# Fused memory attention and gated feed-forward: two visits to the halved array per quad of heads in place of three, and a third P tile

## The chip, the cores and the metric

One core of a Trainium2 chip runs the whole kernel. The metric is device time in microseconds for one execution; lower is better.

## The reference, cut to what matters

Two branches share the input x (2048 x 640, float32) and are mixed by a gate per row.

```python
q, k, v = x@wq, x@wk, x@wv            # 32 heads of 20, 4 segments of 512 rows
for s in range(4):                    # per segment and head
    logits = qs @ ks.T * 20**-0.5 + causal_mask
    a_dot  = softmax(logits) @ vs
    a_mem  = (phi(qs) @ M) / (phi(qs) @ z + 1e-6)
    o      = g * a_mem + (1 - g) * a_dot        # g = sigmoid(beta), per head
    M, z   = M + phi(ks).T @ vs, z + phi(ks).sum()
a = o @ wo
b = (silu(x@w1) * (x@w3)) @ w2        # 640 -> 1728 -> 640
out = gate * a + (1 - gate) * b       # gate = sigmoid(x . gate_w)
```

## The kernel before, in words

All matmuls go through TensorE (PE), whose order is the order of the program; the other engines' orders are chosen by a scheduler when the program is built. Two streams share PE.

**The projection stream** is made of generators: q, k and v blocks, the memory's read and write, feed-forward up (`g`, `u`) and down (`f`), and the output projection (`op`). Inputs and weights are split into a high and a low part (`split`: a cast on ACT, L115, and a subtraction on POOL, L116), and each product takes three passes over 5 blocks, so one group is 15 matmuls of 128 rows into one PSUM bank. A generator yields some hundreds of nanoseconds of planned work at a time, and `step` takes the next piece.

**The attention stream** (`attention`) walks over 128 (segment, head) units in quads of 4, that is two pairs. Each of its passes m has 40 slots (L722 and on), and the main loop (L932 and on) takes projection pieces in each slot, as much as the plan's credit allows. In some slots, listed in `VISITS`, the stream visits PE. A pair has its two heads at partitions 0 and 64 of one `qk` tile, so their matmuls run side by side on the two halves of the array's rows. For a quad there are

- five `s_fill`s: logits q by k, two PSUM banks each, from which VectorE takes row maxima (L579);
- `max_rows`: the maxima are split, turned and written by four small DMAs of POOL's queue (L595) into two more rows of the `qk` tiles, so that the next product already has the maximum subtracted;
- five `t_fill`s: logits k by q, two banks each; ACT takes the exponential into the pair's P tile (L613), POOL zeroes what the mask excludes (L617);
- one `pv_quad`: P times V for four heads, 32 matmuls (L627), each using 32 of the array's columns, into one bank; the result is copied out (L631) to `oq`, which has one buffer, and stored to DRAM (L633). It is read back later as `oall`.

A fill holds 512 columns per half: one full block, or two or more smaller ones. Before the change the three visits of pass m are: slot 5 with s 0 and s 1 of quad m, `pv_quad` of quad m-2, t 0 and t 1 of quad m-1; slot 17 with s 2, t 2, s 4; slot 29 with s 3, t 3, t 4. The loads of the next quad (`load_pair`) stand at slots 20 and 36. P has two tiles, tag `P32`.

PSUM's 8 banks are handed out in turn by `bank_tile`: a free bank is taken from the front of the list and put back at its end; a bank of a projection group in progress is kept out of the list (`held`) until `filled` returns it. A bank that is handed out again makes PE wait until its last reader is done. Before a visit the main loop goes on with up to 4 pieces of projection work, until the open group has come far enough.

Of the kernel before, what the change touches and what calls it, by code (L numbers as in the profile page):

```python
# [25 lines left out]
BIG = -1.0e38  # L26
NST, NW, NRAW, NHT, NVG, NB = 4, 6, 2, 6, 2, 8
RH, LEAD = 3 * DH, 20
NP, AGE = 2, 4
LAG = 5  # L30
EARLY = range(2, 6)
OUT = {4: (0,), 5: (1,), 6: (2, 3)}
# [5 lines left out]
def gated_mix(ctx: ExitStack, tc: tile.TileContext, xT, wqk, wv, w13, w2, w2h, wo, beta, out):  # L38
    nc = tc.nc
# [8 lines left out]
    od = [dp.tile([H, 32, L], F32, name=f"od{c}") for c in range(NSEG)]  # L48
# [69 lines left out]
    free, held = list(range(NB)), {}  # L118

    def bank_tile(name, hold=None):  # L120


        k = free.pop(0)
        ps = pp.tile([P, L], F32, tag=f"b{k}", name=name, bufs=1)
        if hold:
            held[k] = -hold
        else:
            free.append(k)
        return ps
# [146 lines left out]
    def stores(now=False):  # L276
        for e in list(late):
            e[0] -= 1
            if now or e[0] <= 0:
                e[4].dma_start(e[1], e[2])  # L280
                stored.add(e[3])
                late.remove(e)
# [167 lines left out]
    def job_q(cs, mb, alloc={}):  # L450
        i = w_add(wqk[mb], D)
        return [(3.5, q_block(c, mb, i, alloc.get(c))) for c in cs]

    def job_q2(cs, mb, alloc={}):

        i = w_add(wqk[mb], D)
        j = w_add(wqk[mb + 1], D)
        return [(3.5, q_block(c, m, k, alloc.get(c), j if c == cs[-1] and m > mb else i))
                for c in cs for m, k in ((mb, i), (mb + 1, j))]
# [80 lines left out]
    def load_pair(p):  # L540

        j = 2 * p
        c, h = divmod(j, H)
        t = qk[p % NST]
        for mb in {DH * h // P, (DH * h + 2 * DH - 1) // P}:
            assert ("q", c, mb) in stored and ("k", c, mb) in stored
        assert ("v", c, 3) in stored
        for i in range(2):
            here(nc.gpsimd.dma_start(t[64 * i:64 * i + RH], qkd[c][RH * (h + i):RH * (h + i + 1)]))
        if h % 8 == 0:  # L550
            bank["v"] = v = vg[j // 8 % NVG]
            here(nc.sync.dma_start(v[:, :, :VG], vd[c][:, :, VE * h:VE * h + VG]))
        if p % 2 == 0:
            bank["m"] = sp.tile([P, 16], F32, tag="m", name=f"m{j}", bufs=2)
        for i in range(2):
            o = VE * (h % 8 + i)
            heads[j + i] = dict(c=c, h=h + i, v=bank["v"][:, :, o:o + 32])
        pairs[p] = dict(t=t, m=bank["m"])
# [63 lines left out]
    def pv_quad(p):  # L622

        ps = bank_tile(f"o{p}")
        for kb, (o, n) in enumerate(PSEG):
            for i in range(4):
                nc.tensor.matmul(ps[32 * i:32 * i + 32, kb * P:], heads[2 * p + i]["v"][:, kb],  # L627
                                 pairs[p + i // 2]["P"][:, i % 2, o:o + n],
                                 start=kb == 0, stop=kb == 3, skip_group_check=True)
        ot = sp.tile([P, L], F32, tag="oq", name=f"oq{p}", bufs=1)  # L630
        nc.scalar.copy(ot, ps)  # L631
        c, h = heads[2 * p]["c"], heads[2 * p]["h"]
        nc.scalar.dma_start(od[c][h:h + 4].rearrange("h e n -> (h e) n"), ot)  # L633
        q = p // 2 % 8
        for b in OUT.get(q, ()):
            after(8, o_load, c, b)
        if q == 7:
            after(6 if c < NSEG - 1 else 2, o_sums, c)
# [63 lines left out]
    def after(n, f, *a):  # L702
        soon.append([n, f, a])

    def tick():
        for e in list(soon):
            e[0] -= 1
            if e[0] <= 0:
                soon.remove(e)
                e[1](*e[2])  # L710

    NQUAD = NJ // 4


    VISITS = {5: (("s", 0, 0), ("s", 0, 1), ("o", 2), ("t", 1, 0), ("t", 1, 1)),
              17: (("s", 0, 2), ("t", 1, 2), ("s", 0, 4)), 29: (("s", 0, 3), ("t", 1, 3), ("t", 1, 4))}

    def attention():

        for m in range(-1, NQUAD + 2):  # L720
            for n in range(40):
                if m == -1 and n < 40 - LEAD:  # L722
                    continue

                todo = VISITS.get(n, ()) if m != 1 else {5: VISITS[5][:2], 9: VISITS[5][3:]}.get(n, VISITS.get(n, ()))
                if todo:
                    yield "visit"
                    for kind, q, *f in todo:
                        if 0 <= m - q < NQUAD:
                            if kind == "o":  # L730
                                pv_quad(2 * (m - q))
                            else:
                                (s_fill if kind == "s" else t_fill)(m - q, *f)
                    if n == 29 and 0 <= m < NQUAD:
                        after(4, max_rows, 2 * m)
                elif n in ((20, 34) if m < 0 else (20, 36)) and m + 1 < NQUAD:
                    load_pair(2 * (m + 1) + (n > 20))
                tick()
                yield m

# [132 lines left out]
    q = job_q(B[:1], 0, {2: big_tile})  # L873
# [5 lines left out]
    q = job_q2(B, 3)  # L879
# [20 lines left out]
    for n, (_, g) in enumerate(head):  # L900
# [7 lines left out]
        elif n == 9:  # L908
            gates()
    stores(True)  # L910
    att = attention()

    def begin():

        end, seg = segs.pop(0)
        n = end * 10 + LEAD - slots
        return [end, (d for _, g in seg for d in g), sum(c for c, _ in seg) * 1e3 / n]

    def step(run):
        d = next(run[1], None)  # L920
        if d is not None:
            for k in held:
                held[k] += d
            if not isinstance(d, float):
                stores()
                w_step()
        return d
# [3 lines left out]
    while run:  # L931
        if slots == run[0] * 10 + LEAD:  # L932
            while step(run) is not None:
                pass
            stores(True)
            run = begin() if segs else None
            continue
        if next(att, None) == "visit":

            for _ in range(4):  # L940
                if max(held.values(), default=-1) >= 0:
                    break
                d = step(run)
                if d is None:
                    break
                credit -= d
            next(att)
        slots += 1
        credit += run[2]
        while credit > 0:  # L950
            d = step(run)
            if d is None:
                if not segs:
                    break
                stores(True)
                run = begin()
                continue
            credit -= d
# [56 lines left out]
```

## Time and profile before

| what | value |
|---|---|
| median of 3 runs | 1116.74 us (1116.02 to 1117.21) |
| span of the profiled execution (no other time of it is given) | 1117.6 us |
| PE busy | 1105.9 us, 99% |
| PE weight loads busy | 903.6 us, 81% |
| DVE, ACT, POOL busy | 576.4, 475.8, 543.6 us |
| granted TensorE clock, mean | 0.997 |

PE's rows are read by their starts: in a row of the timeline that merges n matmuls, the first number is the first start, the second the time to the end of the last. Matmuls overlap (one takes 400 ns, the next starts before it ends), so PE shows as busy also where the next matmul starts later than it could; idle time in a table does not show it, the distance between starts does.

### The profile page before, as it was taken

The numbers are of one execution on the slowest core, as the hardware profiler recorded it, in microseconds if no ns is written. First come the engines' busy times: TensorE is split into PE (matmuls) and PEld (weight loads), VectorE is DVE, ScalarE is ACT, GpSimd is POOL, SyncE is SP. The second block draws the span as 40 slices with busy tenths as digits, with TensorE's granted clock in tenths as the row PEclk, the third lists the DMA queues.
The fourth block names the chain that finished last, engine by engine and source line by source line (L and its number), as shares of the span: only waits on it lengthen the run. The fifth ranks groups of instructions, "written<-read, shape, count | busy, mean of one in ns | idle before, by whom it ended". The sixth has DMA issues, their size and how long they took to land.

```text
span 1117.6 us, 19428 instructions
## 1 busy us (share of the span) xinstructions
PE 1105.9 (99%) x6953; PEld 903.6 (81%) x6953; DVE 576.4 (52%) x1718; ACT 475.8 (43%) x988; POOL 543.6 (49%) x731
## 2 busy tenths in 40 slices
PE   9999999999999999999999999999999999999998
PEld 6988887877877888878977776788778778877988
DVE  5022474355555554556244566874556665651544
ACT  6265334544244243265355644535543354344040
POOL 4153346466366353445264446645764555465140
PEclk8999999999999999999999999999999999999999
DMA  8265843334254323525377866446644333442122
GB/s 303 96 218 202 277 120 84 92 101 114 67 139 116 81 57 119 144 86 176 111 240 238 273 207 165 108 116 186 176 122 107 83 104 104 110 120 76 49 60 95
DMA packets 85808, 152.00 MB, mean 136 GB/s; under 512 B 19920, under 2 KB 32720, under 8 KB 85712
## 3 DMA queue, kind: packets, MB, share of 16 engines
q1 hardware_dynamic: 55920, 95.01, 26.6%
q0 software_dynamic: 22880, 41.86, 15.1%
q10 hardware_dynamic: 6912, 13.90, 3.3%
q8 instruction: 55, 0.90, 0.3%
q14 instruction: 41, 0.34, 0.1%
HBM read 95.25 MB, written 54.53 MB: 134 GB/s over the span
## 4 chain that ended last, share of the span: by engine, by line
PE 89%; issue 3%; DVE 2%; DMA 2%; POOL 2%; ACT 1%; SPq 0%; POOLq 0%; ACTq 0%; DVEq 0%
PE f L523 17%; PE g L261 16%; PE u L261 15%; PE q L261 6%; PE o L627 6%; PE k L261 6%; PE v L372 5%; PE s L572 5%; PE op L769 5%; PE t L607 4%; PE nd L339 2%; PE pm L426 1%; DMA qk<-mr 1%; POOL W L116 1%; DVE junk L579 1%
## 5 line engine op out<-in xcount | busy, mean ns | idle before, releaser
L579 DVE CUSTOM_DVE_ANT_0 junk<-s,mask 128x384 bf16<-128x384 f32 (+3 forms) x512 | 250.9, 490 | 136.9 <-PE s L572 102.2
L116 POOL TENSOR_TENSOR W<-wr,W 128x640 fp32r<-128x640 f32 (+1 forms) x126 | 197.6, 1573 | 194.8 <-ACT W L115 155.1
L613 ACT ACTIVATE P<-t 128x512 f32<-128x512 f32 (+1 forms) x384 | 171.6, 535 | 101.1 <-PE t L607 101.0
L617 POOL TENSOR_SCALAR_AFFINE_SELECT P<-P 128x256 f32<-128x256 f32 (+1 forms) x192 | 93.4, 493 | 248.5 <-ACT P L613 246.2
L261 PE MATMUL g<-X,W 128*128 128x512 f32 x840 | 213.8, 400 | 0.0
L523 PE MATMUL f<-W,ht 128*128 128x320 f32 x1312 | 202.5, 312 | 0.3 <-POOL W L116 0.3
L261 PE MATMUL u<-X,W 128*128 128x512 f32 x780 | 199.1, 400 | 0.7 <-DVE m L579 0.7
L523 PEld LDWEIGHTS f<-W,ht 128*128 128x128 f32 x1312 | 194.4, 189 | 4.3 <-POOL W L116 0.6
L261 PEld LDWEIGHTS g<-X,W 128*128 128x128 f32 x840 | 154.4, 188 | 36.7
L261 PEld LDWEIGHTS u<-X,W 128*128 128x128 f32 x780 | 143.6, 188 | 35.4 <-DVE m L579 1.2
L115 ACT CAST W<-wr 128x640 fp32r<-128x640 f32 (+1 forms) x133 | 95.4, 731 | 92.1 <-PE u L261 29.8
L531 DVE SCALAR_TENSOR_TENSOR acc<-f,cgate,acc 128x320 f32<-128x320 f32 x128 | 69.4, 548 | 42.5 <-PE f L523 42.0
L116 POOL TENSOR_TENSOR ht<-ft,ht 128x512 fp32r<-128x512 f32 x52 | 67.0, 1289 | 47.9 <-ACT ht L115 47.6
L595 POOL DMA_DIRECT2D qk<-mr x128 | 73.3, 575 | 31.1 <-DVE mr L590 24.4
L261 PE MATMUL q<-X,W 128*128 128x512 f32 x300 | 77.4, 411 | 1.5 <-ACT X L115 0.7
L261 PE MATMUL k<-X,W 128*128 128x512 f32 x300 | 76.8, 402 | 0.0
L492 DVE SCALAR_TENSOR_TENSOR fu<-ft,g 128x512 f32<-128x512 f32 x52 | 35.7, 687 | 77.7 <-ACT ft L491 69.0
L627 PE MATMUL o<-P,vg 128*32 128x512 f32 (+3 forms) x1024 | 75.5, 436 | 0.0
L769 PE MATMUL op<-W,oT 128*128 128x320 f32 x480 | 75.2, 313 | 0.0
L769 PEld LDWEIGHTS op<-W,oT 128*128 128x128 f32 x480 | 71.2, 189 | 1.6
L372 PE MATMUL v<-W,X 128*128 128x320 f32 (+1 forms) x480 | 71.8, 311 | 0.0
L372 PEld LDWEIGHTS v<-W,X 128*128 128x128 f32 x480 | 71.1, 189 | 0.4
(106 smaller groups left out, 1115.9 us busy)
## 6 DMA issues: line engine op xcount, KB each, us to landing
qk<-qkd POOLq DMA_DIRECT2D x128, 240.0 KB, 3.9
wr<-in_w_dram SPq DMA_DIRECT2D x80, 320.0 KB
qkd<-qs SPq DMA_DIRECT2D x20, 512.0 KB
qkd<-ks SPq DMA_DIRECT2D x20, 512.0 KB
od<-oq ACTq DMA_DIRECT2D x32, 256.0 KB
wr<-in_wo_dram SPq DMA_DIRECT2D x20, 320.0 KB
vg<-vd SPq DMA_DIRECT2D x16, 336.0 KB
xr<-in_xT_dram SPq DMA_DIRECT2D x20, 256.0 KB
```

The costliest lines, as they stand in the source:

```text
L115: pin(nc.scalar.copy(dst[:, 0], src))
L116: (lo or nc.gpsimd.tensor_sub)(dst[:, 1], src, dst[:, 0].bitcast(F32))
L261: nc.tensor.matmul(ps, w[:, a, kb * P:(kb + 1) * P], x[:, b, kb, :], start=n == 0, stop=n == 14)
L372: nc.tensor.matmul(ps[:, :n1 - n0], x[:, a, kb, lb * P:(lb + 1) * P], wvt[kb][:, b, n0:n1], start=n == 0, stop=n == 14)
L523: nc.tensor.matmul(ps[:, :320], a, b, start=n == 0, stop=n == len(ms) - 1)
L531: nc.vector.scalar_tensor_tensor(dst, ps[:, :320], cgate[:, c, lb:lb + 1], dst, op0=ALU.mult, op1=ALU.add)
L579: nc.vector.tensor_tensor_reduce(out=junk[:, :w], in0=ps[i][:, o:o + w], in1=mask[:, L - w:], scale=1.0, scalar=-3.0e38, op0=ALU.add, op1= ...
L595: after(3 + 8 * k, lambda d=dst, r=r: here(nc.gpsimd.dma_start(d, mr[r:r + 8])))
L613: last["exp"] = nc.scalar.activation(pairs[2 * m + k]["P"][:, i, o:o + n], ps[i][:, b:b + n], AF.Exp, scale=SCALE)
L617: nc.gpsimd.affine_select(d, d, pattern=[[0, 2], [0, n], [1, P]], base=0, channel_multiplier=-1, compare_op=ALU.is_ge, fill=0.0)
L627: nc.tensor.matmul(ps[32 * i:32 * i + 32, kb * P:], heads[2 * p + i]["v"][:, kb], pairs[p + i // 2]["P"][:, i % 2, o:o + n], start=kb == 0 ...
L769: nc.tensor.matmul(ps[:, :320], oT[0][:, qb % 2, a, kb * P:(kb + 1) * P], ws[kb][:, b, 320 * hf:320 * hf + 320], start=n == 0, stop=n == 14)
```

## The change

- `VISITS` has two entries in place of three. Slot 5 (`BIG`): s 0 of quad m, t 0 and t 1 of quad m-1, `pv_quad` of quad m-2, then t 3, s 2, t 2, s 1. Slot 25 (`SMALL`): s 3, t 4, s 4. All 7 fills and the output of the large visit take 15 banks.
- Where a visit has 4 parts or more, the main loop goes on with up to 8 pieces until no projection group is open, and the visit stands between two groups; smaller ones stand in a group as before.
- `load_pair` stands at slots 12 and 28, `max_rows` is called from slot 25.
- P has three tiles. The descriptor area of POOL's DMAs shrinks from its default, which is 16384 bytes per partition, to 4096.
- The output of P times V is copied out by VectorE, not ACT, and stored through SyncE's queue, not ACT's.

```diff
-NP, AGE = 2, 4
+NP, AGE = 3, 4
@@ pv_quad
-        nc.scalar.copy(ot, ps)
+        nc.vector.tensor_copy(ot, ps)
-        nc.scalar.dma_start(od[c][h:h + 4].rearrange("h e n -> (h e) n"), ot)
+        nc.sync.dma_start(od[c][h:h + 4].rearrange("h e n -> (h e) n"), ot)
@@
-    VISITS = {5: (("s", 0, 0), ("s", 0, 1), ("o", 2), ("t", 1, 0), ("t", 1, 1)),
-              17: (("s", 0, 2), ("t", 1, 2), ("s", 0, 4)), 29: (("s", 0, 3), ("t", 1, 3), ("t", 1, 4))}
+    BIG, SMALL = 5, 25
+    VISITS = {BIG: (("s", 0, 0), ("t", 1, 0), ("t", 1, 1), ("o", 2), ("t", 1, 3), ("s", 0, 2), ("t", 1, 2), ("s", 0, 1)),
+              SMALL: (("s", 0, 3), ("t", 1, 4), ("s", 0, 4))}
@@ attention
-                todo = VISITS.get(n, ()) if m != 1 else {5: VISITS[5][:2], 9: VISITS[5][3:]}.get(n, VISITS.get(n, ()))
+                todo = VISITS.get(n, ()) if m != 1 else {BIG: VISITS[BIG][:3], BIG + 6: VISITS[BIG][4:]}.get(n, VISITS.get(n, ()))
+                todo = [(kind, m - q, f) for kind, q, *f in todo if 0 <= m - q < NQUAD]
                 if todo:
-                    yield "visit"
+                    yield "amid" if len(todo) < 4 else "between"
...
-                    if n == 29 and 0 <= m < NQUAD:
+                    if n == SMALL and 0 <= m < NQUAD:
                         after(4, max_rows, 2 * m)
-                elif n in ((20, 34) if m < 0 else (20, 36)) and m + 1 < NQUAD:
-                    load_pair(2 * (m + 1) + (n > 20))
+                elif n in ((24, 36) if m < 0 else (BIG + 7, SMALL + 3)) and m + 1 < NQUAD:
+                    load_pair(2 * (m + 1) + (n > BIG + 7 if m >= 0 else n > 24))
@@ main loop
-        if next(att, None) == "visit":
-            for _ in range(4):
-                if max(held.values(), default=-1) >= 0:
+        place = next(att, None)
+        if isinstance(place, str):
+            for _ in range(4 if place == "amid" else 8):
+                if (max(held.values(), default=-1) >= 0) if place == "amid" else not held:
                     break
@@ kernel
-    nc = _bacc.Bacc("TRN2", target_bir_lowering=False, num_devices=1)
+    nc = _bacc.Bacc("TRN2", target_bir_lowering=False, num_devices=1, dynamic_dma_scratch_size=4096)
```

More of the change, by code (lines that the diff above doesn't have):

```diff
@@ L723, in attention @@
                     continue
-                todo = VISITS.get(n, ()) if m != 1 else {5: VISITS[5][:2], 9: VISITS[5][3:]}.get(n, VISITS.get(n, ()))
+                todo = VISITS.get(n, ()) if m != 1 else {BIG: VISITS[BIG][:3], BIG + 6: VISITS[BIG][4:]}.get(n, VISITS.get(n, ()))
+                todo = [(kind, m - q, f) for kind, q, *f in todo if 0 <= m - q < NQUAD]
                 if todo:
-                    yield "visit"
[L728 to L733, printed above, removed]
-                    if n == 29 and 0 <= m < NQUAD:
+                    yield "amid" if len(todo) < 4 else "between"
+                    for kind, q, f in todo:
+                        if kind == "o":
+                            pv_quad(2 * q)
+                        else:
+                            (s_fill if kind == "s" else t_fill)(q, *f)
+                    if n == SMALL and 0 <= m < NQUAD:
                         after(4, max_rows, 2 * m)
-                elif n in ((20, 34) if m < 0 else (20, 36)) and m + 1 < NQUAD:
-                    load_pair(2 * (m + 1) + (n > 20))
+                elif n in ((24, 36) if m < 0 else (BIG + 7, SMALL + 3)) and m + 1 < NQUAD:
+                    load_pair(2 * (m + 1) + (n > BIG + 7 if m >= 0 else n > 24))
                 tick()
```

## Prediction

> **What bounds the kernel now.** I read the page first, then PE's own waits, then PE in order of time around single visits.
>
> ```profile
> span 1117.6 us, 19428 instructions
> PE 1105.9 (99%) x6953; PEld 903.6 (81%) x6953; DVE 576.4 (52%) x1718; ACT 475.8 (43%) x988; POOL 543.6 (49%) x731
> PE 89%; issue 3%; DVE 2%; DMA 2%; POOL 2%; ACT 1%; SPq 0%; POOLq 0%; ACTq 0%; DVEq 0%
> ...
> PE t L607 <- DMA qk<-mr: 1.4, 2, 0.9
> PE t L607 <- DVE X L141: 0.8, 1, 0.8
> PE t L607 <- DVE pq L295: 0.7, 1, 0.7
> ```
>
> PE is busy 99% and carries 89% of the chain that ended last. Its waits for other engines inside visits are the last three rows, 2.9 us together. So the time is PE's, and what counts is how far apart matmuls start where none of them waits. Three visits, with the projection group on both sides:
>
> ```profile
> 140.74 1.31 PE L261 MATMUL g<-X,W 128*128 128x512 f32 x5
> 141.97 0.50 PE L572 MATMUL s<-qk 60*128 60x256 f32 x4
> 142.41 0.96 PE L261 MATMUL g<-X,W 128*128 128x512 f32 x3
> ...
> 1024.65 1.33 PE L261 MATMUL u<-X,W 128*128 128x512 f32 x5
> 1025.91 0.73 PE L607 MATMUL t<-qk 62*128 62x512 f32 x6
> 1026.58 2.37 PE L261 MATMUL u<-X,W 128*128 128x512 f32 x9
> 1028.79 1.54 PE L261 MATMUL g<-X,W 128*128 128x512 f32 x6
> ...
> 397.82 0.50 PE L572 MATMUL s<-qk 60*128 60x512 f32 x2
> 398.16 0.40 PE L607 MATMUL t<-qk 62*128 62x256 f32 x4
> 398.40 0.40 PE L572 MATMUL s<-qk 60*128 60x384 f32 x4
> 398.72 0.97 PE L261 MATMUL u<-X,W 128*128 128x512 f32 x3
> ```
>
> They hold one, two and three fills and last 0.44, 0.67 and 0.90 us (142.41 - 141.97, and so on): 0.23 a fill and a constant 0.21 that does not depend on the number. The constant is not all. One matmul alone lasts 0.40 us; a row of 5 that lasts 1.33 has four steps in 0.93, 0.232 each. So the last u before the middle visit starts at 1025.58 and its follower is due at 1025.81; the visit starts at 1025.91, 0.10 late. Behind it, nine u take 1028.79 - 1026.58 = 2.21 us where nine steps are 2.09: 0.12 more. A visit therefore costs 0.10 + 0.21 + 0.11 = **0.42 us, taken as 0.40**, beside its columns, in both changes of the array's division, with no wait shown.
>
> **Part 1, fewer visits.** Passes 0 to 32 make three visits each before, pass 1 a fourth, pass 33 one: 101. After, two each, pass 1 a third, pass 33 one: 68, which is also what I count in the order in which the changed program's instructions stand. 33 x 0.40 = **13.2 us saved**. The fills and matmuls stay the same, and so do the two further divisions around P times V:
>
> ```profile
> 385.14 0.73 PE L572 MATMUL s<-qk 60*128 60x512 f32 x6
> 385.81 2.36 PE L627 MATMUL o<-P,vg 128*32 128x512 f32 x32
> 388.10 0.73 PE L607 MATMUL t<-qk 62*128 62x512 f32 x6
> 388.76 1.42 PE L261 MATMUL u<-X,W 128*128 128x512 f32 x5
> ...
> 385.68 0.69 DVE L579 CUSTOM_DVE_ANT_0 junk<-s,mask 128x512 bf16<-128x512 f32 x1 [0.53 <-PE s L572]
> 386.52 0.69 DVE L579 CUSTOM_DVE_ANT_0 junk<-s,mask 128x512 bf16<-128x512 f32 x1
> 388.24 0.59 ACT L631 COPY oq<-o 128x512 f32<-128x512 f32 x1 [3.02 <-PE o L627]
> 388.72 0.60 ACT L613 ACTIVATE P<-t 128x512 f32<-128x512 f32 x1
> 239.44 2.06 ACT L613 ACTIVATE P<-t 128x512 f32<-128x512 f32 x4 [0.95 <-PE t L607]
> ```
>
> **Part 2, the large visit's 15 banks out of 8.** No visit before needs as many, so its waits are worked out from the rows above, time 0 being its first matmul. Three fills (s 0, t 0, t 1) take 0.34 + 0.24 + 0.32 = 0.90; the output starts then and takes 2.29; t 3 starts at 3.19, s 2 at 3.53, t 2 at 3.77, s 1 at 4.01, and the next group at 4.33. Banks come round after eight. Those of s 0 are read by VectorE from 0.54, 0.84 apart, free by 2.1, and wanted at 3.19 and 3.53. Those of t 0 and t 1 are read by ACT from 0.34 + 0.62 = 0.96, four in 2.06, free by 3.0, and wanted from 3.53 to 4.01: 1.0 us to spare. The output's own bank is wanted by s 1's second half at 4.01. Its copy starts 2.43 after the output's first matmul, at 3.33. On VectorE no such copy is shown; the bounds are ACT's copy and a VectorE operation of that size that reads PSUM:
>
> ```profile
> L631 ACT COPY oq<-o 128x512 f32<-128x512 f32 x32 | 18.8, 587 | 122.4 <-PE o L627 122.4
> L690 DVE TENSOR_TENSOR oall<-oall,rr 128x512 f32<-128x512 f32 x20 | 13.7, 683 | 10.3 <-PE rr L689 10.3
> ...
> 499.72 0.69 DVE L141 TENSOR_TENSOR X<-xr,xh 128x512 fp32r<-128x512 f32 x1 [0.94 <-ACT xh L140]
> 500.46 0.50 PE L607 MATMUL t<-qk 62*128 62x384 f32 x4 [0.78 <-DVE X L141]
> ```
>
> I take 0.68, VectorE's own row: it ends at 4.01, and PE follows a release by 0.05 (500.41 to 500.46): 4.06, a wait of 0.05 (nothing at 0.59). The Trainium skill (VectorE: DVE Perf Modes, "Why PSUM operands drop a tier") states that a float32 operand in PSUM keeps VectorE at one element per cycle; by that page's clock, 0.96 GHz, 512 elements are an estimated 0.53 us before overhead, and with 0.53 the wait would vanish, 1.5 us over 30 visits. No run here shows it yet.
>
> The next group takes the bank of t 3's first half: exponential from 3.19 + 0.62 for 0.60, free at 4.46, wanted at 4.38: 0.08. Together about 0.1 per full large visit, of which there are 30: **3.0 us added**.
>
> **Part 3, visits that start with the other engines laden.** The order of the changed program shows what stands ahead of the visit's reads.
>
> ```profile
> L288 ACT CAST qs<-q 128x512 fp32r<-128x512 f32 x20 | 11.8, 589 | 30.7 <-PE q L261 30.7
> L291 ACT ACTIVATE phi_t<-q 128x512 f32<-128x512 f32 x15 | 9.1, 607 | 0.0
> L292 ACT ACTIVATE phi_t<-phi_t 128x512 f32<-128x512 f32 x30 | 19.4, 645 | 0.3
> L295 DVE SCALAR_TENSOR_TENSOR pq<-q,phi_t 128x512 f32<-128x512 f32 x15 | 10.3, 689 | 2.8 <-ACT phi_t L292 2.7
> L115 ACT CAST W<-wr 128x640 fp32r<-128x640 f32 x123 | 88.4, 731 | 89.2 <-PE u L261 29.8 <-PE op L769 16.8 <-PE f L523 16.6
> ```
>
> Three visits (quads 13, 14, 16) follow a q or k group. ACT has 0.59 + 0.61 + 0.65 of that group between the first exponentials, so VectorE's L295 frees its bank near 3.75, wanted at 3.19: 0.55 each, 1.65. In quad 14 two weight casts (0.73 each) also stand ahead of t 3's exponentials: 1.1. In two others (29, 31) one stands there: 0.65 each, 1.3. Three are followed by `normalize`, whose second bank is t 3's other half: 0.2 each, 0.6. **4.65 us added.** After g, u and f groups (most of the others) at most one cast stands ahead, which the spare 1.0 covers; with two casts it is gone, at up to 0.5 a visit.
>
> **Part 4, loads, maxima, stores.**
>
> ```profile
> 247.47 2.29 PE o L627 x32
> 273.05 2.29 PE o L627 x32
> ...
> DMA to landing us min/median/max: 1.6/2.9/5.7
> ...
> SPq L172 <- POOL W L116: 540.5, 100, 26.9
> ```
>
> A quad takes 25.6 us, so a slot outside visits is 0.5 us. The second pair's maxima are issued 6 slots, 3 us, ahead of the large visit and first used by t 3 at 3.19: 6.2 us against a landing (second row, of L595) of 2.9, at most 5.7. The first pair's stand 14 slots ahead (10 before). Where POOL is late I allow **1.0 us**. The store of the output now queues on SP, behind weight loads that waited 5.4 us each in the mean and 26.9 at most; only a delay of nearly a quad would hold the next copy, since `oq` has one buffer: nothing, or some 2 us once. What queues behind the store's own wait are weight loads made some 6 splits ahead: nothing. ACT loses 18.8 us of copies and DVE gains 32 x 0.68 = 22, both at about half load: nothing. Three P tiles let t 0's and t 1's exponentials run before the old P is read; they remove a wait that the new order would otherwise make, and gain nothing by themselves. The smaller descriptor area moves addresses: nothing, if it holds what is in flight (below).
>
> **The sum.** -13.2 + 3.0 + 4.65 + 1.0, and of the 2.9 us that visits waited before, which other neighbours now replace, all taken off: -7.45. The profile's 1117.6 is a span, 0.9 above the median, and I take the difference off the median: 1116.74 - 7.45 = **1109.3 us**.
>
> **The rivals.**
> - *Evacuation holds the large visit (slower).* A visit of 4.33 us makes ACT read four t fills (239.44: 2.06 for two full ones, so about 4) and VectorE three s fills and the copy, about 6. If ACT comes 1.5 to 2 us late as a rule (two weight casts and the previous group's activation ahead of it), s 1 and the next group wait 0.5 to 1.0 more in each of 30 visits. The point is 13.2 / 30 = 0.44 us a visit; at 0.8 it is 24 - 13.2 + 5, some **1132 us** with part 3's waits. For it: 15 banks out of 8, and the copy moved onto the longer of the two queues. Against it: in most visits of the changed order the copy stands right behind s 0's maxima, and ACT has at most one cast first. The Trainium skill (TensorEngine Tiling, "PSUM Bottleneck") warns of this: dividing the array speeds TensorE, not the emptying of PSUM, which may become the limit. The visits before, with at most 9 banks, show four such or other waits (the rows above) and so neither bear it out nor refute it.
> - *The savings are eaten (no change).* The same waits at 0.3 to 0.45 a visit: 1115 to 1118.
> - *The small descriptor area stalls POOL.* If it did not hold a quad's four loads, POOL would stand for landings and t 0 would wait for its maxima, say 1 us a quad: +32 - 7, **1142 us**. Nothing in the profile shows its size in use.
> - *The 0.40 is not a cost of the visit* but of the matmuls beside it, and stays: 1116.74 + 8.65 - 2.9, **1122 us**. Against: it is the same constant with one, two and three fills.
>
> **Chances.** Forecast with its spread 0.80; eaten 0.08; evacuation 0.08; area 0.02; cost stays 0.02. About 0.2%, 2.2 us, is what a measurement of this kernel can tell from no change. The forecast's own low end: no new wait but part 3's half, 1116.7 - 13.2 - 2.9 + 2 = 1102.6; its high end: 0.3 us a large visit, 1115.5. Of the forecast's 0.80, 0.02 lies within 0.2%, with the eaten case's 0.08; the other three are slower: faster 0.78, same 0.10, slower 0.12. The range 1102.5 to 1115.5 leaves out the rivals.
>
> **What would show it.** Right: 68 visits; a large visit of 4.3 to 4.5 us from its first matmul to the next group; its copy near 0.68 us; `s 1` waiting for the copy by about 0.05. Wrong: large visits over 4.8 us as a rule, PE waiting on L613 or L631, POOL's DMAs (L549, L595) longer than now.

## The result, and the profile after

| kernel | median | ratio to before, 95% interval |
|---|---|---|
| before | 1116.85 us (1116.02 to 1117.21) | |
| changed | 1132.76 us (1131.58 to 1134.49) | 1.0145, 1.0131 to 1.016 |

The change costs 15.9 us, where a time 7.4 below before's was forecast; 1132.76 lies outside the range. The profiled execution took 1131.89 us, its span is 1130.2, 12.6 more than before's. The page of the changed kernel, and PE's own waits (total, times, longest, us):

```profile
span 1130.2 us, 19408 instructions
PE 1104.6 (98%) x6953; PEld 911.7 (81%) x6953; DVE 590.3 (52%) x1750; ACT 463.7 (41%) x956; POOL 539.3 (48%) x731
PE 86%; issue 4%; DVE 3%; DMA 3%; POOL 2%; ACT 2%; SPq 0%; POOLq 0%; DVEq 0%; ACTq 0%
...
PE t L607 <- DMA qk<-mr: 11.2, 7, 3.3
PE f L523 <- DVE X L141: 2.4, 1, 2.4
```

PE is a little less busy in a longer span, and one row of its waits has grown from 1.4 to 11.2 us: t fills that wait for the DMAs which write the split row maxima into the `qk` tiles. First a large visit without that wait, rows picked from the timeline (start, length in us):

```profile
250.94 0.50 PE L572 MATMUL s<-qk 60*128 60x512 f32 x2
251.28 0.63 PE L607 MATMUL t<-qk 62*128 62x512 f32 x6
251.84 2.36 PE L627 MATMUL o<-P,vg 128*32 128x512 f32 x32
254.13 0.50 PE L607 MATMUL t<-qk 62*128 62x512 f32 x2
254.27 0.69 DVE L631 COPY oq<-o 128x512 f32<-128x512 f32 x1 [0.89 <-PE o L627]
254.47 0.39 PE L572 MATMUL s<-qk 60*128 60x512 f32 x2
254.70 0.40 PE L607 MATMUL t<-qk 62*128 62x256 f32 x4
254.94 0.57 PE L572 MATMUL s<-qk 60*128 60x384 f32 x4
255.44 0.96 PE L261 MATMUL u<-X,W 128*128 128x512 f32 x3
```

255.44 - 250.94 = 4.50, and the median of the 32 is 4.51, with 4.33 of matmuls and 0.1 of waits forecast. Each start up to s 1 (254.94, 4.00 in) stands where it was worked out; s 1 itself takes 0.50 with the copy's release at 254.96 inside it, in place of 0.32. Now the longest one, 10.0 us, from the small visit that computes its maxima on (rows picked again):

```profile
767.66 0.51 PE L572 MATMUL s<-qk 60*128 60x256 f32 x4
768.24 0.62 PE L572 MATMUL s<-qk 60*128 60x384 f32 x4
769.67 1.07 POOL L549 DMA_DIRECT2D qk<-qkd  x2
771.72 1.01 POOL L549 DMA_DIRECT2D qk<-qkd  x2
771.93 0.29 DVE L579 CUSTOM_DVE_ANT_0 junk<-s,mask 128x128 bf16<-128x128 f32 x1
772.26 0.20 ACT L139 CAST ns<-m 128x16 fp32r<-128x16 f32 x1 [0.74 <-DVE m L579]
773.21 0.84 DVE L590 STREAM_TRANSPOSE mr<-ns 32x32 f32<-32x32 f32 x4
774.35 2.19 POOL L595 DMA_DIRECT2D qk<-mr  x4 [1.61 <-DVE mr L590]
776.23 0.47 PE L572 MATMUL s<-qk 60*128 60x512 f32 x1
777.39 0.46 PE L572 MATMUL s<-qk 60*128 60x512 f32 x1 [0.69 <-DMA qk<-qkd]
780.48 1.22 PE L607 MATMUL t<-qk 62*128 62x512 f32 x6 [2.62 <-DMA qk<-mr]
781.63 3.37 PE L627 MATMUL o<-P,vg 128*32 128x512 f32 x32
```

The small visit starts at 767.66; VectorE reads its eight maxima until 772.2; the split, the turn and POOL's issue follow one another; the DMAs are issued from 774.35, while t 0 is due 0.34 us behind 776.23. They land behind two loads of `qk<-qkd`, the first row 5.8 us behind its issue, and PE stands; the second half of s 0 has waited for such a load too, 0.69 us. In the next pass, which has the longest wait, the DMAs are not slow but are issued too late, when the visit has begun:

```profile
802.44 0.50 PE L572 MATMUL s<-qk 60*128 60x512 f32 x2
802.92 2.19 POOL L595 DMA_DIRECT2D qk<-mr  x4 [0.57 <-DVE fu L492]
806.25 0.73 PE L607 MATMUL t<-qk 62*128 62x512 f32 x6 [3.31 <-DMA qk<-mr]
```

They land 3.1 us behind their issue and less. The first of these two passes before the change (the view ends at 775, so its last row has 16 of the output's 32 matmuls):

```profile
765.38 0.50 PE L572 MATMUL s<-qk 60*128 60x256 f32 x4
768.48 0.23 ACT L139 CAST ns<-m 128x16 fp32r<-128x16 f32 x1
770.60 1.16 POOL L595 DMA_DIRECT2D qk<-mr  x2 [1.30 <-DVE mr L590]
773.07 0.74 PE L572 MATMUL s<-qk 60*128 60x512 f32 x6
773.74 1.71 PE L627 MATMUL o<-P,vg 128*32 128x512 f32 x16
```

There the last visit held of the s fills only s 3 (s 4 had been read 12 slots earlier), so the cast came 3.10 us behind the visit's start, not 4.60; and t 0 stood behind s 0, s 1 and the output, some 3 us into the visit. From issue to use there were 773.07 + 2.96 - 770.60 = 5.4 us; now 776.23 + 0.34 - 774.35 = 2.2, against landings of 1.6 to 5.8 us. Even so this pass waited 0.52 us for maxima before, one of the two waits in the 1.4 us.

What such a wait costs beyond its length is in the table by stretches (from:to, us, busy time and count of PE, its weight loads, DVE, ACT and POOL, the granted clock, DMA share, GB/s):

```profile
148.80:155.60 6.80, 6.38 (x21) 5.25 (x22) 0.69 (x1) 3.38 (x6) 3.58 (x4) 0.50 0.11 31
776.00:780.30 4.30, 1.15 (x4) 0.37 (x2) 1.40 (x4) 0.53 (x1) 0.53 (x2) 1.00 0.68 132
780.30:783.70 3.40, 3.23 (x18) 1.49 (x22) 0.00 (x0) 2.06 (x4) 0.65 (x2) 0.50 0.00 0
807.60:811.00 3.40, 3.40 (x30) 1.37 (x24) 0.16 (x1) 1.28 (x3) 0.84 (x2) 0.50 0.00 0
711.00:716.00 5.00, 3.83 (x39) 1.85 (x40) 2.44 (x6) 2.68 (x5) 3.89 (x6) 1.00 0.04 4
```

Behind three waits for maxima (2.4 us at 147, 2.6 at 778, 3.3 at 803) the clock is halved for 6.8, 3.4 and 3.4 us: the output at 781.63 takes 3.37 us in place of 2.36. Half of 13.6 us, an estimated 6.8, is lost. Behind a wait of 1.2 us at 712 it stays at 1.00.

### The profile page after: what moved, and what is told of

It reads as the page before. It is cut to its first block, busy times and chain, and to the rows that moved or that the text cites. A ratio compares the mean times of both kernels' runs of the same rounds, so it can differ in the third digit from the quotient of the medians.

```text
span 1130.2 us, 19408 instructions
## 1 busy us (share of the span) xinstructions
PE 1104.6 (98%) x6953; PEld 911.7 (81%) x6953; DVE 590.3 (52%) x1750; ACT 463.7 (41%) x956; POOL 539.3 (48%) x731
## 4 chain that ended last, share of the span: by engine, by line
PE 86%; issue 4%; DVE 3%; DMA 3%; POOL 2%; ACT 2%; SPq 0%; POOLq 0%; DVEq 0%; ACTq 0%
PE g L261 16%; PE u L261 15%; PE f L523 14%; PE v L372 6%; PE k L261 6%; PE q L261 6%; PE o L627 6%; PE op L770 4%; PE s L572 4%; PE t L607 4%; DMA qk<-mr 2%; DVE junk L579 1%; PE pm L426 1%; PE nd L339 1%; ACT P L613 1%
## 5 line engine op out<-in xcount | busy, mean ns | idle before, releaser
L579 DVE CUSTOM_DVE_ANT_0 junk<-s,mask 128x256 bf16<-128x256 f32 (+3 forms) x512 | 250.6, 490 | 112.7 <-PE s L572 81.7
L613 ACT ACTIVATE P<-t 128x512 f32<-128x512 f32 (+1 forms) x384 | 171.9, 539 | 134.1 <-PE t L607 129.6
L261 PE MATMUL g<-X,W 128*128 128x512 f32 x840 | 211.4, 400 | 0.3 <-ACT P L613 0.2
L261 PE MATMUL u<-X,W 128*128 128x512 f32 x780 | 195.8, 399 | 0.1
L617 POOL TENSOR_SCALAR_AFFINE_SELECT P<-P 128x256 f32<-128x256 f32 x192 | 93.3, 494 | 194.7 <-ACT P L613 194.5
L595 POOL DMA_DIRECT2D qk<-mr x128 | 70.8, 558 | 52.5 <-DVE mr L590 46.0
L572 PE MATMUL s<-qk 60*128 60x256 f32 (+3 forms) x512 | 76.9, 344 | 1.7 <-DVE fu L492 1.0
L627 PE MATMUL o<-P,vg 128*32 128x512 f32 (+3 forms) x1024 | 78.1, 447 | 0.1
L607 PE MATMUL t<-qk 62*128 62x256 f32 (+3 forms) x512 | 63.7, 327 | 11.9 <-DMA qk<-mr 11.2
L261 PE MATMUL q<-X,W 128*128 128x512 f32 x300 | 73.8, 399 | 0.8 <-DVE X L116 0.6
```

Of the source, the lines that this page charges most:

```text
L261: nc.tensor.matmul(ps, w[:, a, kb * P:(kb + 1) * P], x[:, b, kb, :], start=n == 0, stop=n == 14)
L572: nc.tensor.matmul(ps[i][:, o:o + w], q[:, qb * P:(qb + 1) * P], key[:, :w], start=n == 0, stop=n == len(todo) - 1, skip_group_check=True)
L579: nc.vector.tensor_tensor_reduce(out=junk[:, :w], in0=ps[i][:, o:o + w], in1=mask[:, L - w:], scale=1.0, scalar=-3.0e38, op0=ALU.add, op1= ...
L607: nc.tensor.matmul(ps[i][:, o:o + L - kb * P], key[:, kb * P:(kb + 1) * P], q[:, kb * P:], start=n == 0, stop=n == len(todo) - 1, skip_gro ...
L613: last["exp"] = nc.scalar.activation(pairs[2 * m + k]["P"][:, i, o:o + n], ps[i][:, b:b + n], AF.Exp, scale=SCALE)
L617: nc.gpsimd.affine_select(d, d, pattern=[[0, 2], [0, n], [1, P]], base=0, channel_multiplier=-1, compare_op=ALU.is_ge, fill=0.0)
```

## The experiments

**Is it the maxima?** The maxima rows are left out of the t fills (60 rows of contraction, not 62), so that nothing waits for them; the exponentials are then without their maximum.

```diff
-                q, key = (u["t"][64 * i:64 * i + RH + 2, w] for w in range(2))
+                q, key = (u["t"][64 * i:64 * i + RH, w] for w in range(2))
```

> The t fills contract over 60 rows and leave out the two rows that hold the row maxima, so nothing on PE waits for the small DMAs of L595; order, fills and DMAs are those of the changed kernel. Theory A (the maxima arrive late at the large visit, PE waits 11.2 us for them and loses some 5 us more to the halved clock that follows): 1114 to 1119 us. Theory B (the 15 banks of the large visit are the cost): not more than 3 us below the changed kernel's 1132.8, so 1130 or more.

Measured: 1115.44 us, ratio 0.999 (0.9981 to 1.0), and the row of `qk<-mr` is gone from PE's waits. The maxima and what follows from them are 1132.76 - 1115.44 = 17.3 us, more than the whole loss. (The two profiled spans differ by 16.4: 11.2 of waits and 6.8 of half clock, less 1.7 for one halved stretch of 3.4 us that only the run without maxima has.) But the other half of the question opens: without them the change still brings only 1 us of its forecast 7.

**Would an earlier small visit do?** Four slots, seven slots and ten slots earlier; the second load of the next quad, three slots behind the small visit, moves with it:

```diff
-    BIG, SMALL = 5, 25
+    BIG, SMALL = 5, 21    # and 18, and 15
```

> The small visit stands at slot 18, not 25, some 3 us earlier ahead of the next large visit. Theory A: nearly all waits for the maxima go (the longest is 3.3 us): 1115 to 1121 us. Theory B: the small visit comes while the large one's banks are still being read, so no gain or a loss: 1131 to 1136.

> The changed kernel with the small visit in slot 21 in place of 25, so that the maxima start about 2 us earlier. Theory A (maxima of t 0 late by some us in a few dense passes, plus the half clock behind those waits): of the lateness of 4.1, 3.7, 1.5 and 1.1 us two waits of 1.4 to 1.8 stay, 3 us, and one window of half clock or none: between 1115 and 1120, on the way from 1132.8 to the 1113.0 of slot 18. Rival B (the loss is spread over all large visits, and slot 18 won for another reason): 1120 to 1126, halfway.

> The small visit in slot 15 in place of 25, else the changed kernel. Theory A: the 2.3 us that t 0 still waited for maxima with slot 18 go, the rest stays: 1110 to 1112.3. Rival (the small visit then comes too close behind the large one, and its readers or the earlier load of the second pair pay for it): 1113 to 1117.

| small visit in slot | median us | ratio to before, 95% interval | t waits for maxima, us |
|---|---|---|---|
| 25 | 1132.76 | 1.0145 (1.0131 to 1.016) | 11.2 in 7 |
| 21 | 1116.05 | 0.9994 (0.9985 to 1.0002) | 3.7 in 3 (of its longest execution, 1119.78) |
| 18 | 1112.96 | 0.9967 (0.9957 to 0.9978) | 2.3 in 2 |
| 15 | 1117.05 | 1.0006 (0.9995 to 1.0018) | 0.7 in 1 |

Two us of margin take away most of the loss, and slot 18, better than its Theory A by 2 us, is a third of a per cent faster than the kernel before. Slot 15 missed what was expected and is nearer to the rival's range. Its waits for maxima are nearly gone, but the profile shows others, the largest being

```profile
PE nd L339 <- ACT P L613: 2.6, 1, 2.6
```

a memory read that waits for a bank whose exponential ACT has not read yet. Its profiled span is 1113.4, 2.0 above slot 18's 1111.4; the medians differ by 4.1. The granted clocks on record account for the rest as far as they go: slot 15's profiled execution, its fastest, has 1.000, the ten others 0.995 to 0.998, where slot 18's nine have 0.998 to 1.000; 0.002 of 1115 us is 2.2. Why slot 15 loses clock more often stays open.

**Do the other parts cost anything?** Three visits as before, with three P tiles, the small descriptor area, the copy on VectorE and the store on SP.

```diff
-NP, AGE = 2, 4
+NP, AGE = 3, 4
-        nc.scalar.copy(ot, ps)
+        nc.vector.tensor_copy(ot, ps)
-        nc.scalar.dma_start(od[c][h:h + 4].rearrange("h e n -> (h e) n"), ot)
+        nc.sync.dma_start(od[c][h:h + 4].rearrange("h e n -> (h e) n"), ot)
-    nc = _bacc.Bacc("TRN2", target_bir_lowering=False, num_devices=1)
+    nc = _bacc.Bacc("TRN2", target_bir_lowering=False, num_devices=1, dynamic_dma_scratch_size=4096)
```

> Three visits as before the change, but with the third P tile, the smaller descriptor area, the copy on VectorE and the store on SyncE's queue. Theory A: none of these costs anything by itself: 1115 to 1118 us. A rival, that the small descriptor area or the store behind weight loads delays POOL or SP: 1121 or more.

Measured: 1115.27 us, ratio 0.999 (0.9981 to 1.0). Nothing, as forecast. It is also the right neighbour of the run without maxima, 1115.44: with everything else equal and the maxima out of the way, two visits are as fast as three in the median. The clock has a part in that: at a granted clock of 1.000 the run without maxima took 1112.95 and 1114.33 us, the run of three visits 1114.95 to 1115.71.

**Then is the 0.40 us of a visit not a cost?** The kernel before, with its middle visit cut in two.

```diff
-              17: (("s", 0, 2), ("t", 1, 2), ("s", 0, 4)), 29: (("s", 0, 3), ("t", 1, 3), ("t", 1, 4))}
+              17: (("s", 0, 2), ("t", 1, 2)), 21: (("s", 0, 4),), 29: (("s", 0, 3), ("t", 1, 3), ("t", 1, 4))}
```

> The kernel before with the middle visit cut in two: s 2 and t 2 stay in slot 17, s 4 moves to a visit of its own in slot 21. 32 visits more (133), the same fills. Theory C (the prediction's first step: a visit costs 0.40 us whatever it holds, and merging failed to bring that back for other reasons): 1116.8 + 32 x 0.40 = 1129.6, between 1127 and 1132. Theory D (what comparing the run without maxima with the run of three visits suggests, 4.75 us of entry and exit over 33 visits, 0.14 each; the inner constant does not go with a visit): 1116.8 + 4.6 = 1121, between 1119 and 1123.

Measured: 1127.52 us against 1116.46, ratio 1.0099 (1.0086 to 1.0112). 11.06 / 32 = 0.35 us a visit; 29 of the 32 stand apart from another visit in the trace, by which it is 0.38. Theory C was nearly right: a visit has its price. So two visits save it and lose most of it again in longer visits (the sizes are in the next section).

**The bank of the output.** First with the copy on ACT and the store in ACT's queue, as before the change; in slot 25 and in slot 18.

```diff
-        nc.vector.tensor_copy(ot, ps)
+        nc.scalar.copy(ot, ps)
-        nc.sync.dma_start(od[c][h:h + 4].rearrange("h e n -> (h e) n"), ot)
+        nc.scalar.dma_start(od[c][h:h + 4].rearrange("h e n -> (h e) n"), ot)
```

> The output of P times V is copied by ACT and stored through ACT's queue, as before the change; all else is the changed kernel. Theory A: only the wait of s 1 for the copy changes, 30 times 0.17 us at most: 1127 to 1133. Theory B: if the copy on VectorE is what holds the banks, 1120 or less; if ACT is the fuller engine there, above 1134.

> The small visit in slot 18, and the output copied by ACT and stored through ACT's queue as in the kernel before. Theory A (copying on ACT lost 12 us beside the changed kernel only because maxima that had no margin came later still, their DMAs landing later): with margin, s 1 does not wait for the copy, t 3's exponential ends 0.03 later: 1111.5 to 1114, the same as the 1113.0 with the copy on VectorE. Rival (ACT's queue is the cost itself): 1117 or more, with large visits over 4.6 us as a rule.

Measured: 1145.09 us in slot 25 (1.0247, 1.0225 to 1.027) and 1119.21 in slot 18 (1.0033, 1.0021 to 1.0045); 12.3 and 6.3 slower than with VectorE and SP. Theory A missed both times. The times lie in the ranges of the rivals (above 1134, 1117 or more), but the sign named for slot 18 did not come: the typical large visit is no longer (median 4.51 and 4.47 us). The maxima land later: `t <- qk<-mr` is 17.6 us in slot 25. Around the longest wait, 4.4 us, the timeline has two issues on SP that the changed kernel does not make there:

```profile
775.45 0.78 SPq L657 DMA_DIRECT2D oall<-od  x1
776.26 0.79 SPq L659 DMA_DIRECT2D oall<-od  x1
776.36 1.01 POOL L549 DMA_DIRECT2D qk<-qkd  x2
778.28 2.19 POOL L595 DMA_DIRECT2D qk<-mr  x4 [0.91 <-DVE mr L590]
```

The reading back of the stored output is issued 2 us ahead of the maxima, whose second row lands 7.9 us behind its issue (5.4 in the changed kernel). To tell that from ACT's copy, the copy alone on ACT, SP's order the changed kernel's:

> The changed kernel (small visit in slot 25) with the copy of the output on ACT, the store left on SP; SP's order is then the changed kernel's own. The run with copy and store on ACT took 1145.1, with the maxima's rows landing up to 7.9 us behind their issue, beside loads of the stored output that SP issued in the same microseconds. Theory A (there the store's place was the cost: SP, no longer held by stores, issues the loads of the output ahead of the maxima's small DMAs): as the changed kernel, 1131 to 1134, or 1 less for s 1's wait. Rival B (ACT's copy is the cost, by s 1 waiting for it where ACT is laden and by t 3's exponentials): 1141 to 1146.

Measured: 1134.88 us (1130.3 to 1142.2; ratio 1.017, 1.0111 to 1.0229). Its profile has the loads where the changed kernel has them, behind the store:

```profile
776.02 2.19 POOL L595 DMA_DIRECT2D qk<-mr  x4 [1.80 <-DVE mr L590]
787.43 0.33 SPq L633 DMA_DIRECT2D od<-oq  x1
787.81 0.80 SPq L657 DMA_DIRECT2D oall<-od  x1
```

and waits 10.9 us for maxima, not 17.6. The median is 0.9 above Theory A's range and 6 below Rival B's, so Theory A holds for most of it: a store that waits at the head of SP's queue keeps the loads behind it off the DMA engines in the microseconds in which the maxima need them. The interval is wide, so that 1 or 2 us of ACT's copy itself are not excluded; in slot 18 such waits show (s 1 for the copy on ACT, 1.6 us in 3 visits), beside 4.2 us for maxima in place of 2.3 and two halved stretches of 3.4 us that slot 18's own profile does not have.

**Half the copy on each engine**, slot 18:

```diff
-        nc.vector.tensor_copy(ot, ps)
+        nc.vector.tensor_copy(ot[:, :256], ps[:, :256])
+        nc.scalar.copy(ot[:, 256:], ps[:, 256:])
```

> The small visit in slot 18, and the copy of the output cut in two: the first 256 columns on VectorE, the other 256 on ACT, side by side, store on SP as in the changed kernel. Theory A: the bank is free 0.35 us earlier, s 1's second half no longer waits, its pair runs side by side again, and the next group follows at 4.44 us, when t 3's exponential lets its bank go, in place of 4.51: 30 x 0.07 = 2 us, 1111 (1110 to 1112.2). Rival: ACT's half delays t 3's exponential, for whose bank the next group waits, and nothing is gained: 1112.5 to 1115.

Measured: 1131.4 us (1.0131, 1.0118 to 1.0144), 18.4 slower than the undivided copy, where 2 faster was expected.

```profile
PE s L572 <- ACT oq L632: 12.6, 30, 1.0
...
873.76 0.50 PE L607 MATMUL t<-qk 62*128 62x512 f32 x2
873.90 0.42 DVE L631 COPY oq<-o 128x256 f32<-128x256 f32 x1 [1.22 <-PE o L627]
874.36 0.60 ACT L613 ACTIVATE P<-t 128x512 f32<-128x512 f32 x1 [0.89 <-PE t L607]
874.85 0.37 ACT L632 COPY oq<-o 128x256 f32<-128x256 f32 x1
875.27 0.50 PE L572 MATMUL s<-qk 60*128 60x384 f32 x3 [0.36 <-ACT oq L632]
875.70 1.00 PE L523 MATMUL f<-W,ht 128*128 128x320 f32 x5
```

ACT did not copy beside VectorE: in its order t 3's exponential comes first, and its half begins when that is done. The bank is free at 875.2, where VectorE alone had it free 4.03 us into the visit, 874.60. All 30 full visits wait, their median is 5.13 in place of 4.51, and 30 x 0.62 = 18.6 is the loss. The Trainium skill (PSUM — Partial Sum Buffer, "PSUM bank collisions raise a hardware error") states that two engines may not access one bank and the same partitions at once, reads included, so that halves by columns have to follow one another anyway; no run here shows such an access. As an experiment it prices the rival of the prediction that was put at 0.08: 0.6 us in each large visit are 18 us.

**Fewer banks.** s 1 moves to the small visit, so that the large one takes 13 banks; slots 18 and 15.

```diff
-              ("t", 1, 3), ("s", 0, 2), ("t", 1, 2), ("s", 0, 1)),
-              SMALL: (("s", 0, 3), ("t", 1, 4), ("s", 0, 4))}
+              ("t", 1, 3), ("s", 0, 2), ("t", 1, 2)),
+              SMALL: (("t", 1, 4), ("s", 0, 1), ("s", 0, 3), ("s", 0, 4))}
```

> The small visit in slot 18, and s 1 moved from the end of the large visit into the small one (t 4, s 1, s 3, s 4, between two groups): 13 banks in the large visit, so that neither the output's bank nor that of t 3 is wanted again inside it or by the next group; 8 in the small one. Theory A (of the large visit's 4.51 us, the second half of s 1 behind the copy and the next group behind t 3's exponential are waits for banks): the large visit ends with t 2, at 4.02, the small one takes 0.96 + 0.24, and up to 0.1 until t 4's exponential frees the next group's bank: 5.25 to 5.3 a quad in place of 5.47, 30 x 0.17 to 0.2 = 5 to 6 us; s 1's four maxima join the chain to the exchanged rows, 1.5 us, and two or three dense passes wait 1 to 2 longer: 1108 to 1112. Rival (banks do not matter at these places, the time is that of the matmuls): 1113 to 1116.

> Both: s 1 in the small visit, and that in slot 15. Theory A: the gain of the 13 banks, 5 to 6 us, with maxima in time: 1106 to 1109. Rival (the two are not independent: with four fills the small visit gives VectorE more to read, and its maxima come late again): 1110 to 1114.

Measured: 1141.83 (1.0235, 1.0215 to 1.0255) and 1141.91 us (1.0221, 1.0207 to 1.0235), 29 and 25 slower than the same slots with s 1 in the large visit. Both theories missed. The large visit ends as expected, at 4.10 (4.02). The small one, with 8 banks of 8, takes 1.53 in slot 18 in the median, not 1.2 to 1.3, and in one of the slower kinds the timeline reads

```profile
851.92 0.50 PE L607 MATMUL t<-qk 62*128 62x384 f32 x4
852.03 0.73 ACT L115 CAST W<-wr 128x640 fp32r<-128x640 f32 x1 [1.88 <-PE u L261]
852.66 1.08 ACT L613 ACTIVATE P<-t 128x512 f32<-128x512 f32 x2
853.79 0.97 PE L261 MATMUL g<-X,W 128*128 128x512 f32 x3 [0.52 <-ACT P L613]
```

a weight cast of 0.73 us that ACT began 0.11 into the visit, with t 4's exponentials behind it, and the next group waiting for their bank. The maxima come 2.9 us later too (the cast that begins the split at 7.45 us behind the small visit's start in a typical pass, not 4.60), so that in slot 18 9.1 us of waits for maxima are back, 6.8 above slot 18's own. These and other waits in and behind the small visit (6.5 us of g groups for t 4's exponentials, 5.7 us of s fills for banks that VectorE's L295 still reads) are followed by 30.7 us at half clock, an estimated 15 lost, where slot 18's profile has none. That profile is of the longest execution, 1147.22 us.

## Why the prediction was wrong, point by point

- **Part 4 failed: maxima, 1.0 us allowed, 17.3 measured** (changed kernel less the run without maxima), by the profiles 11.2 of waits and about 6.8 of half clock behind three of them. Two things in its working were wrong. "14 slots ahead (10 before)" counted slots of the program, where the DMA waits for the chain in front of it, and s 4 had been moved into that chain: the cast comes 4.60 us behind the visit, not 3.10. And t 0 itself was moved, from behind the output to 0.34 us into the visit; the part asked when t 3 is due and never when t 0 is. In the dense passes the small and the large visit are 8.6 us apart, of which the chain and a landing take all. The row that warned of it stood in the prediction's first view: before, t already waited 1.4 us for `qk<-mr`, and the sum took that wait off.
- **Part 1: the mechanism was right, its size a little high.** 0.40 forecast, 0.35 to 0.38 measured by the run of four visits: 33 of them are 12, not 13.2. (Its pieces by its own rows are 0.10, 0.21 and 0.12, entered as 0.11.)
- **Part 2: mis-sized by half.** 4.33 and 0.1 forecast, 4.51 measured: 30 x 0.18 = 5.4 us, not 3.0; its own two waits, 0.05 and 0.08, already make 3.9. The copy was right (0.69 against 0.68), and so was the release (s 1's second half at 4.08, 4.06 forecast). Behind the wait of 0.07 s 1's two halves, which run side by side otherwise, follow one another. That is worth 0.04: with the copy on ACT in slot 18 both halves start at 4.00, and the next group still starts at 4.47, released by t 3's exponential, which ends at 4.42. The other 0.14 stand there too. The small visit was in no sum: 0.956 us against 0.905, 1.6 us over 31.
- **Part 3: right in kind, high in size.** Visits behind q and k groups are 1.24, 0.94 and 0.20 longer, one behind the memory's transposes (L411) 0.13, two behind op groups 0.30 and 0.12: 2.9 us against 4.65. These visits wait for no maxima. The three followed by `normalize`, put at 0.2 each, are at most 0.02 longer.
- **"Waits of before, all taken off", -2.9:** others took their place, the 2.4 us of f for X among them, with 3.4 us of half clock in the run without maxima; about nothing is left of it.
- **Right:** 68 visits; three P tiles, descriptor area, copy and store at nothing (tried with three visits).

With the measured sizes the sum is -12 + 5.4 + 1.6 + 2.9 + 17.3 = 15.2, and 15.9 were measured. Without the last term it is -2.1: the change was worth far less than forecast even with its maxima in time, and the runs of two and of three visits (1115.44 and 1115.27) say so. Slot 18's 1112.96 is 2.5 below the run without maxima; it has neither the 2.4 us wait of f nor the half clock behind it.

Of the rivals, only the descriptor area had t 0 wait for its maxima, by a POOL that stands; the issues of L595 are no longer than before (0.56 us in the median, 0.58 before). None had the chain or t 0's new place, and the signs of being wrong did not include them. Evacuation gave the right time, 1132, by luck and for a wrong reason. The typical large visit is 4.51, not over 4.8, and the longest wait for L613 or L631 is 1.1 us, once. Its price was then shown by the divided copy.

What stays open: the longer chain, the earlier use of t 0 and the loads of the next quad, which are now issued ahead of the maxima, were read from the traces and not tried one by one. All are margin, and the slots show that margin is what was missing.

## What to carry to other kernels

When work is merged on the engine that bounds, follow each operand that another engine delivers: when its last producer now ends, when its first consumer now starts, in microseconds of the densest pass, not in slots. The same visit can save its fixed price and give it back through its banks: the more of the accumulator's banks it takes, the more each small delay of a reader becomes a wait. If an operand comes late, first move its producer, in two or three steps: an intermediate place was best here.

## What the runs showed of the hardware that was not expected

- **A pause well below 3.4 us can halve the clock.** Taking all runs together, each of the 12 pauses of PE of 2.6 to 4.4 us is followed, at most 4.7 us after its start, by a stretch at 0.50 that lasts 3.4 us or a multiple; so are 10 of 15 between 2.2 and 2.6 us, 3 of 7 between 1.2 and 2, and 8 of 79 between 0.5 and 1.2 (five of the eight beside a longer one). In the changed kernel one of 2.37 us (147) is and one of 2.39 (506) is not; in the run without maxima the latter's counterpart is. The Trainium skill (TensorE: Matmul & The Clock Gate, "What's actually happening") has the clock halved after at least one idle window of about 3.4 us, counted by a window that runs freely. The lengths, and that like pauses end differently, agree with such windows; that a pause must be as long as one does not. In the ten runs that have several halved stretches they all start whole multiples of 3.413 us apart: in the changed kernel 185 from 148.8 to 780.3, and 8 from there to 807.6.
- **Small DMAs land by what is beside them.** The 4 KB of maxima land 1.6 us behind their issue at best, 2.0 in the median, and 5.8 at most in the changed kernel, 8.3 where the reading back of the output was issued just ahead of them.
- **Half a pair's delay costs a little more than itself.** Where one of s 1's two matmuls on the two halves of the array starts 0.07 us late (4.07 in place of 4.00), the visit's last matmul starts at 4.36 us, and at 4.25 where both start together (the copy on ACT, slot 18): 0.10 later.
